# Computing a per-head denominator with 32-column tiles of the TensorE array, and issuing it later

## The chip, the cores and the metric

The kernel runs on one core of one Trainium2 chip. The metric is device time in microseconds (us). Lower is better. Engines are named as in the profile: PE is TensorE (matmul), PEld its weight loads, DVE is VectorE, ACT is ScalarE, POOL is GpSimd, SP is the engine whose queue issues the DMAs here.

## The reference, cut to what matters

One transformer block with linear attention and a gated feed-forward network, both added to the input. There are 2048 tokens, width 640, 32 heads of 20, feed-forward width 1728.

```python
pq, pk = phi(q), phi(k)                       # phi(t) = t+1 if t>0 else exp(t), + 1e-6
kv  = einsum("bhsd,bhse->bhde", pk, v)
z   = einsum("bhsd->bhd", pk)
num = einsum("bhqd,bhde->bhqe", pq, kv)
den = einsum("bhqd,bhd->bhq", pq, z)[..., None] + 1e-6     # <- one number per head and token
o   = num / den
out = x + o @ wo + (gelu(xn @ w_gate) * (xn @ w_up)) @ w_down
```

The change is about `den`: 32 numbers per token.

## The kernel before

The kernel has two phases. Phase 1 normalizes the tokens, computes k and v, accumulates `kv` and `z`, and computes most of q. A short phase boundary turns `kv` and `wo` into one matrix `M`. Phase 2 goes through four chunks of 512 tokens. A chunk has 13 GU tiles (10 matmuls of 512 columns each: gate and up projection), one smaller tile for the last 64 feed-forward columns (`u_ps`, 5 matmuls), and four OUT tiles (38 matmuls of 320 columns each), which trail by one chunk. The denominator (DEN) and its reciprocal are made in between and are broadcast over the heads through DRAM.

```python
# phi(q): relu part + exp part, done on DVE once per chunk
def emit_pq_combine(c, pin): ...
    for r_ap, e_ap in parts:                    # 5 tiles of pqT, then 40 rows of mix
        after(nc.vector.tensor_scalar(e_ap, e_ap, 1.0, PHI_EPS, op0=ALU.min, op1=ALU.add), pin, ...)
        nc.vector.tensor_tensor(r_ap, r_ap, e_ap, op=ALU.add)

def emit_DEN(c):
    cs = slice(c * CH, (c + 1) * CH)            # CH = 512
    den_ps = small_ps("den_ps")
    for t in range(NQF):                        # NQF = 5; zmat[:, t, :] is 128 columns wide, 32 of use
        nc.tensor.matmul(den_ps[:, :], lhsT=zmat[:QW, t, :], rhs=pqT[:QW, t, cs],
                         start=(t == 0), stop=False)
    nc.tensor.matmul(den_ps[:, :], lhsT=zmat5[:, :], rhs=mix[:, cs], start=False, stop=True)
    den_sb = work2.tile([H, CH], F32, tag="den_sb", name="den_sb", bufs=2)      # H = 32
    nc.scalar.activation(den_sb[:], den_ps[:H, :], ACT.Identity, bias=DEN_EPS)

# emit_recip: 4 pieces of 32 x 128 on DVE.  emit_BC_dma: one store of 1/den, then 8 broadcast loads.

# phase 2: small pieces of work are spread over the slots between GU tiles
if c == 0:
    rest.append(lambda: emit_pq_combine(0, pins["gu"]))
    rest.append(lambda: emit_DEN(0))
    rest += [(lambda p=p: emit_recip(0, p)) for p in range(NRP)]
    rest.append(lambda: emit_BC_dma(0))
if c + 1 < NCH:
    rest.append(lambda: emit_pq_combine(c + 1, pins["gu"]))
    rest.append(lambda: emit_DEN(c + 1))
    ...
```

A scheduler orders the emitted instructions on each engine. What counts is therefore the order that the trace shows, not the order of the code. (Where a text below speaks of the compiled program, the kernel of that run was built again, without the chip, and its instructions and waits were listed.)

## Time and profile before

| | before |
|---|---|
| time | 307.31 us median of 4 runs (306.52 to 308.31) |
| PE busy | 294.5 of 306.6 us |
| DEN matmuls on PE | 24 of 512 columns |
| PE idle recorded before DEN matmuls | 0.7 us |
| reciprocals on DVE | 16, mean 905 ns |

The busy table of the page for the kernel before (busy us, share of the span, number of instructions), and the first line of its chain of waits (the shares of the work that ended last):

```profile
PE 294.5 (96%) x1815; PEld 167.3 (55%) x1815; DVE 148.9 (49%) x303; ACT 92.4 (30%) x187; POOL 7.2 (2%) x32
...
PE 84%; DVE 10%; DMA 2%; ACT 2%; SPq 1%; issue 1%; DVEq 0%; ACTq 0%
```

TensorE bounds this kernel. DVE and ACT are idle at least half of the time.

The groups of instructions that the change touches. The columns are: line, engine, operation, output and inputs with their shapes, count | busy us, mean ns of one | idle us of the engine just before them and what ended most of it:

```profile
L435 PE MATMUL den_ps<-pqT,zmat 120*128 120x512 bf16 x20 | 7.3, 378 | 0.7 <-DVE pqT L347 0.7
L437 PE MATMUL den_ps<-mix,zmat 128*128 128x512 bf16 x4 | 1.5, 376 | 0.0
L439 ACT ACTIVATE den_sb<-den_ps 32x512 f32<-32x512 f32 x4 | 2.3, 587 | 8.5 <-PE den_ps L437 8.5
L448 DVE RECIPROCAL rden<-den_sb 32x128 bf16<-32x128 f32 x16 | 13.8, 905 | 1.1 <-ACT den_sb L439 1.1
```

A matmul of 512 columns is recorded as 378 ns, but that is its length from start to end, and matmuls overlap. The cost on a busy TensorE is the distance from one start to the next. The PE timeline around the first chunk's DEN shows this (start us, length us, engine, line, output and inputs, shapes, count, idle before):

```profile
103.23 0.38 PE L494 MATMUL gu<-xnT,wu_sb 128*128 128x512 bf16 x1
103.45 0.38 PE L491 MATMUL gu<-xnT,wg_sb 128*128 128x512 bf16 x1
104.00 0.38 PE L435 MATMUL den_ps<-pqT,zmat 120*128 120x512 bf16 x1 [0.17 <-DVE pqT L347]
104.21 0.38 PE L491 MATMUL gu<-xnT,wg_sb 128*128 128x512 bf16 x1
104.45 0.38 PE L437 MATMUL den_ps<-mix,zmat 128*128 128x512 bf16 x1
```

From 103.23 to 103.45 is 0.22 us, the price of 512 columns. (Five of them in a row take 1.08 us, so 216 ns each.) The DEN matmuls stand scattered between GU matmuls, each as soon as the scheduler expected its `pqT` tile to be ready.

### The profile page before, as it was taken

What the parts mean: (1) busy time and instruction counts of PE and PEld (TensorE: products, weight loads), DVE (VectorE), ACT (ScalarE), POOL (GpSimd) and SP (SyncE); (2) the same over time, 40 slices, a digit from 0 to 9 for tenths busy, and PEclk for the clock granted to TensorE, in tenths of its full rate; (3) what the DMA queues carried; (4) which work ended last, traced back from release to release, by engine and by line L of the source; (5) the groups of instructions that cost most, each with busy time, mean ns of one, the idle gap of its engine ahead of it and who ended that gap; (6) DMA issues with size and microseconds to landing.
All of it is one profiled execution on the core that took longest, in us unless ns stands there. A gap on an engine that the chain in (4) does not pass through costs nothing.

```text
span 306.6 us, 4493 instructions
## 1 busy us (share of the span) xinstructions
PE 294.5 (96%) x1815; PEld 167.3 (55%) x1815; DVE 148.9 (49%) x303; ACT 92.4 (30%) x187; POOL 7.2 (2%) x32
## 2 busy tenths in 40 slices
PE   6599999999989999999999999999999999999995
PEld 2256656566654444445655645466464564665773
DVE  5567867676354997678252239324223212223121
ACT  4245666575577322321021031201213012012000
POOL 3003200000000000000000000000000000000000
PEclk9989999999999999999999999999999999999999
DMA  7988970000002022132211010410100101101101
GB/s 221 269 308 285 240 275 24 21 2 0 0 2 65 0 52 45 29 57 70 60 50 43 0 44 2 126 45 8 43 27 18 43 2 43 41 4 43 43 24 43
DMA packets 17421, 20.81 MB, mean 68 GB/s; under 512 B 3513, under 2 KB 15481, under 8 KB 17401
## 3 DMA queue, kind: packets, MB, share of 16 engines
q1 hardware_dynamic: 17401, 20.54, 22.5%
q8 instruction: 14, 0.23, 0.3%
q14 instruction: 6, 0.05, 0.0%
HBM read 17.78 MB, written 2.75 MB: 67 GB/s over the span
## 4 chain that ended last, share of the span: by engine, by line
PE 84%; DVE 10%; DMA 2%; ACT 2%; SPq 1%; issue 1%; DVEq 0%; ACTq 0%
PE o_ps L520 26%; PE gu L494 16%; PE gu L491 16%; PE q_ps L317 7%; PE kp L280 6%; PE vp L280 5%; DVE pqT L347 2%; DMA x<-in_A_x_dram 2%; PE kp L281 1%; DVE hT L498 1%; PE u_ps L481 1%; PE kv_acc L302 1%; DVE eT L345 1%; PE vp L281 1%; PE tp L269 1%; PE q_ps L324 1%
## 5 line engine op out<-in xcount | busy, mean ns | idle before, releaser
L497 ACT ACTIVATE ge<-gu 128x512 bf16<-128x512 f32 x52 | 31.1, 597 | 138.8 <-PE gu L494 137.2
L498 DVE TENSOR_TENSOR hT<-ge,gu 128x512 bf16<-128x512 bf16 x52 | 35.4, 682 | 62.7 <-ACT ge L497 62.4
L491 PE MATMUL gu<-xnT,wg_sb 128*128 128x512 bf16 x260 | 65.4, 379 | 0.4 <-DVE M_sb L427 0.4
L494 PE MATMUL gu<-xnT,wu_sb 128*128 128x512 bf16 x260 | 65.4, 379 | 0.0
L520 PE MATMUL o_ps<-wd_sb,hT 128*128 128x320 bf16 x416 | 59.3, 299 | 0.0
L520 PEld LDWEIGHTS <-hT 128*128 128x128 bf16 x416 | 40.6, 98 | 16.1
L494 PEld LDWEIGHTS <-wu_sb 128*128 128x128 bf16 x260 | 25.4, 98 | 31.3 <-issue 1.0
L491 PEld LDWEIGHTS <-wg_sb 128*128 128x128 bf16 x260 | 25.4, 98 | 29.6 <-issue 1.2
L529 DVE TENSOR_TENSOR res<-o_ps,xr 128x640 bf16<-128x640 f32 x15 | 12.4, 825 | 51.5 <-PE o_ps L520 51.5
L280 PE MATMUL kp<-wqkv_sb,xnT 128*128 128x512 bf16 x80 | 24.9, 392 | 2.5 <-DMA wqkv_sb<-in_A_wqkv_dram 1.4
L520 PE MATMUL o_ps<-M_sb,pqT 120*128 120x320 bf16 x160 | 26.1, 299 | 0.6 <-DVE res L539 0.6
L280 PEld LDWEIGHTS <-xnT 128*128 128x128 bf16 x160 | 16.0, 100 | 18.1 <-issue 1.6
L280 PE MATMUL vp<-wqkv_sb,xnT 128*128 128x512 bf16 x80 | 24.0, 386 | 0.0
L317 PE MATMUL q_ps<-xnT,wqkv_sb 128*120 128x512 bf16 x100 | 23.9, 379 | 0.0
L520 PEld LDWEIGHTS <-pqT 120*128 120x128 bf16 x160 | 15.6, 97 | 10.3 <-issue 1.8
L281 PE MATMUL kp<-wqkv_sb,xnT 128*128 128x128 bf16 x80 | 18.0, 225 | 0.0
L281 PE MATMUL vp<-wqkv_sb,xnT 128*128 128x128 bf16 x80 | 17.7, 221 | 0.0
L281 PEld LDWEIGHTS <-xnT 128*128 128x128 bf16 x160 | 16.0, 100 | 3.1 <-issue 3.1
L317 PEld LDWEIGHTS <-wqkv_sb 128*120 128x120 bf16 x100 | 12.4, 133 | 7.6
L243 DVE BATCH_NORM_STATS2 stats<-x 128x6 f32<-128x320 bf16 x32 | 14.0, 480 | 4.3 <-DMA x<-in_A_x_dram 4.3
L448 DVE RECIPROCAL rden<-den_sb 32x128 bf16<-32x128 f32 x16 | 13.8, 905 | 1.1 <-ACT den_sb L439 1.1
L287 ACT ACTIVATE e_k<-kp 128x640 bf16<-128x640 f32 x16 | 11.2, 702 | 10.0 <-PE kp L281 9.9
(90 smaller groups left out, 219.1 us busy)
## 6 DMA issues: line engine op xcount, KB each, us to landing
x<-in_A_x_dram SPq DMA_DIRECT2D x16, 160.0 KB
xr<-in_A_x_dram SPq DMA_DIRECT2D x16, 160.0 KB
rb<-rden_d SPq DMA_DIRECT2D x24, 100.0 KB
out_dram<-res SPq DMA_DIRECT2D x15, 160.0 KB
wg_sb<-in_B_w_gate_dram SPq DMA_DIRECT2D x5, 416.0 KB
wu_sb<-in_B_w_up_dram SPq DMA_DIRECT2D x5, 416.0 KB
wd_sb<-in_B_w_down_dram SPq DMA_DIRECT2D x4, 480.0 KB
wqkv_sb<-in_A_wqkv_dram SPq DMA_DIRECT2D x5, 320.0 KB
```

Of the source, the lines that this page charges most:

```text
L243: ins = nc.vector.bn_stats(stats[:, j, :], x_t[:, j * h2:(j + 1) * h2])
L280: nc.tensor.matmul(dst[:, 0, :], lhsT, wqkv_sb[:, k, base:base + 512], start=st, stop=sp)
L281: nc.tensor.matmul(dst[:, 1, 0:rem], lhsT, wqkv_sb[:, k, base + 512:base + D], start=st, stop=sp)
L287: nc.scalar.activation(e[:], kflat, ACT.Exp)
L317: nc.tensor.matmul(q_ps[:QW, :], lhsT=wqkv_sb[:, k, t * QW:(t + 1) * QW], rhs=xnT[:, k, cs], start=(k == 0), stop=(k == KD - 1),)
L448: nc.vector.reciprocal(rden[:, c % 2, sl], den_sbs[c][:, sl])
L491: nc.tensor.matmul(gu[:, 0, :], lhsT=wg_sb[:, k, f * P:(f + 1) * P], rhs=xnT[:, k, cs], start=(k == 0), stop=(k == KD - 1))
L494: nc.tensor.matmul(gu[:, 1, :], lhsT=wu_sb[:, k, f * P:(f + 1) * P], rhs=xnT[:, k, cs], start=(k == 0), stop=(k == KD - 1))
L497: nc.scalar.activation(ge[:, :], gu[:, 0, :], ACT.Gelu_apprx_tanh)
L498: return nc.vector.tensor_tensor(hT[:, f, :], ge[:, :], gu[:, 1, :], op=ALU.mult)
L520: nc.tensor.matmul(o_ps[:, hf, 0:HB], lhsT=lhsT, rhs=rhs[:, hf * HB:(hf + 1) * HB], start=(n == 0), stop=(n == len(groups) - 1),)
L529: nc.vector.tensor_tensor(res[:].rearrange("p (a b) -> p a b", a=2), o_ps[:, :, 0:HB], xr[:].rearrange("p (a b) -> p a b", a=2), op=ALU.add,)
```

## The change

The intent is to waste less of the array on the denominator. DEN needs 32 output rows, but its stationary operand `zmat` is 128 columns wide, so 96 of the 128 output rows are of no use. The change narrows `zmat` to 32 columns, splits the chunk into four quarters of 128 tokens, and sends each quarter to another column tile of the array (`tile_position=(0, 32j)`), so that four matmuls can run side by side. The result then lies on 128 partitions, 128 wide, in place of 32 partitions, 512 wide, so the reciprocal on DVE has a quarter of the columns to go through. It is done in two pieces per chunk in place of four (`NRP`). Further, DEN is issued later (empty padding slots) and in one piece (a pin on the last combine of the chunk). Two more options, `EARLY_GU` and `WK_FIRST`, come with the change but are switched off; their code is cut here.

```diff
-    zmat = pers.tile([P, NQF, P], BF16, name="zmat")
-    zmat5 = pers.tile([P, P], BF16, name="zmat5")
-    rden = pers.tile([H, 2, CH], BF16, name="rden")
+    zmat = pers.tile([P, NQF, H], BF16, name="zmat")
+    zmat5 = pers.tile([P, H], BF16, name="zmat5")
+    NSUB = P // H
+    SW = CH // NSUB
+    rden = pers.tile([P, 2, SW], BF16, name="rden")
 ... (et, et5: the same narrowing; pq_combine: pins["combine"] = its last instruction)
     def emit_DEN(c):
-        for t in range(NQF):
-            nc.tensor.matmul(den_ps[:, :], lhsT=zmat[:QW, t, :], rhs=pqT[:QW, t, cs],
-                             start=(t == 0), stop=False)
-        nc.tensor.matmul(den_ps[:, :], lhsT=zmat5[:, :], rhs=mix[:, cs], start=False, stop=True)
-        den_sb = work2.tile([H, CH], F32, tag="den_sb", name="den_sb", bufs=2)
-        nc.scalar.activation(den_sb[:], den_ps[:H, :], ACT.Identity, bias=DEN_EPS)
+        for t in range(NQF + 1):
+            for j in range(NSUB):
+                cs = slice(c * CH + j * SW, c * CH + (j + 1) * SW)
+                if t < NQF:
+                    lhsT, rhs = zmat[:QW, t, :], pqT[:QW, t, cs]
+                else:
+                    lhsT, rhs = zmat5[:, :], mix[:, cs]
+                mm = nc.tensor.matmul(den_ps[j * H:(j + 1) * H, 0:SW], lhsT=lhsT, rhs=rhs,
+                                      start=(t == 0), stop=(t == NQF), tile_position=(0, j * H))
+                after(mm, pins["combine"], "keep the column-tiled matmuls contiguous")
+        den_sb = work2.tile([P, SW], F32, tag="den_sb", name="den_sb", bufs=2)
+        nc.scalar.activation(den_sb[:], den_ps[:, 0:SW], ACT.Identity, bias=DEN_EPS)
-    NRP = 4
+    NRP = 2
 ... (emit_BC_dma: four stores of 1/den in place of one)
         if c == 0:
             rest.append(lambda: emit_pq_combine(0, pins["gu"]))
+            rest += [lambda: None] * 5
             rest.append(lambda: emit_DEN(0))
         if c + 1 < NCH:
             rest.append(lambda: emit_pq_combine(c + 1, pins["gu"]))
+            rest += [lambda: None] * (3 if c == 0 else 1)
             rest.append(lambda: emit_DEN(c + 1))
```

More of the change, by code (lines that the diff above doesn't have):

```diff
@@ L20 @@
 DVE_RELU_EVERY = 2
+EARLY_GU = False
+WK_FIRST = False
 @with_exitstack
@@ L99, in load_x, with load_w @@
         return t
-    x_tiles[0] = load_x(0)
-    if NT > 1:
-        x_tiles[1] = load_x(1)
     wqkv_sb = work.tile([P, KD, 3 * D], BF16, name="wqkv_sb", bufs=1)
     wqkv_src = A_wqkv.rearrange("(k p) f -> p k f", p=P)
-    for k in range(KD):
-        nc.sync.dma_start(wqkv_sb[:, k, D:3 * D], wqkv_src[:, k, D:3 * D])
-    for i in range(2, min(4, NT)):
-        x_tiles[i] = load_x(i)
+    def load_w(col0, k0, k1):
+        nc.sync.dma_start(wqkv_sb[:, k0:k1, col0:col0 + D], wqkv_src[:, k0:k1, col0:col0 + D])
+    x_tiles[0] = load_x(0)
+    if WK_FIRST:
+        ksplit = min(KD, 2)
+        load_w(D, 0, ksplit)
+        if NT > 1:
+            x_tiles[1] = load_x(1)
+        if ksplit < KD:
+            load_w(D, ksplit, KD)
+        load_w(2 * D, 0, ksplit)
+        if NT > 2:
+            x_tiles[2] = load_x(2)
+        if ksplit < KD:
+            load_w(2 * D, ksplit, KD)
+        if NT > 3:
+            x_tiles[3] = load_x(3)
+    else:
+        if NT > 1:
+            x_tiles[1] = load_x(1)
+        for k in range(KD):
+            nc.sync.dma_start(wqkv_sb[:, k, D:3 * D], wqkv_src[:, k, D:3 * D])
+        for i in range(2, min(4, NT)):
+            x_tiles[i] = load_x(i)
     warm = const.tile([P, 512], BF16, name="warm")
@@ L180 @@
     kvmT = pers.tile([P, NQF + 1, P], BF16, name="kvmT")
-    zmat = pers.tile([P, NQF, P], BF16, name="zmat")
-    zmat5 = pers.tile([P, P], BF16, name="zmat5")
-    rden = pers.tile([H, 2, CH], BF16, name="rden")
+    zmat = pers.tile([P, NQF, H], BF16, name="zmat")
[3 more added lines that the diff above has]
+    rden = pers.tile([P, 2, SW], BF16, name="rden")
     rden_d = dram.tile([H, NCH, CH], BF16, name="rden_d")
-    et = const.tile([P, NQF, P], BF16, name="et")
-    et5 = const.tile([P, P], BF16, name="et5")
+    et = const.tile([P, NQF, H], BF16, name="et")
+    et5 = const.tile([P, H], BF16, name="et5")
     mask_bd = const.tile([P, HPT, DH], F32, name="mask_bd")
@@ L209, in deferred_const_pieces @@
         return [
-            seq(ms(et[:], 1.0), band(et[:], [[QW, NQF], [-DH, P]], 0, 1)),
+            seq(ms(et[:], 1.0), band(et[:], [[QW, NQF], [-DH, H]], 0, 1)),
             seq(ms(et5[:], 0.0), ms(et5[MO:MO + Q5, :], 1.0),
-                band(et5[MO:MO + Q5, :], [[-DH, P]], NQF * QW, 1)),
+                band(et5[MO:MO + Q5, :], [[-DH, H]], NQF * QW, 1)),
             seq(ms(mask_bd[:], 1.0), band(mask_bd[:], [[-DH, HPT], [0, DH]], 0, 1),
@@ L346, in emit_pq_combine @@
                   pin, "phi(q) combine belongs to phase 2")
-            nc.vector.tensor_tensor(r_ap, r_ap, e_ap, op=ALU.add)
+            last = nc.vector.tensor_tensor(r_ap, r_ap, e_ap, op=ALU.add)
+        pins["combine"] = last
     pending_q = deque()
@@ L356 @@
     late_w = deque(late_weight_pieces())
-    pins = {"kvp": None}
+    pins = {"kvp": None, "combine": None}
     for i in range(NT):
@@ L431, in emit_DEN @@
     def emit_DEN(c):
-        cs = slice(c * CH, (c + 1) * CH)
         den_ps = small_ps("den_ps")
-        for t in range(NQF):
-            nc.tensor.matmul(den_ps[:, :], lhsT=zmat[:QW, t, :], rhs=pqT[:QW, t, cs],
-                             start=(t == 0), stop=False)
-        nc.tensor.matmul(den_ps[:, :], lhsT=zmat5[:, :], rhs=mix[:, cs], start=False, stop=True)
-        den_sb = work2.tile([H, CH], F32, tag="den_sb", name="den_sb", bufs=2)
-        nc.scalar.activation(den_sb[:], den_ps[:H, :], ACT.Identity, bias=DEN_EPS)
+        for t in range(NQF + 1):
[3 more added lines that the diff above has]
+                    lhsT, rhs = zmat[:QW, t, :], pqT[:QW, t, cs]
+                else:
+                    lhsT, rhs = zmat5[:, :], mix[:, cs]
[4 more added lines that the diff above has]
+        nc.scalar.activation(den_sb[:], den_ps[:, 0:SW], ACT.Identity, bias=DEN_EPS)
         den_sbs[c] = den_sb
-    NRP = 4
+    NRP = 2
     def emit_recip(c, piece):
-        w = CH // NRP
+        w = SW // NRP
         sl = slice(piece * w, (piece + 1) * w)
-        with nc.allow_low_precision("1/den feeds a bf16 matmul operand"):
+        with nc.allow_low_precision("1/den feeds a bf16 multiply"):
             nc.vector.reciprocal(rden[:, c % 2, sl], den_sbs[c][:, sl])
@@ L452, in emit_BC_dma @@
     def emit_BC_dma(c):
-        nc.sync.dma_start(rden_d[:, c, :], rden[:, c % 2, :])
+        for j in range(NSUB):
+            nc.sync.dma_start(rden_d[:, c, j * SW:(j + 1) * SW], rden[j * H:(j + 1) * H, c % 2, :])
         rb = work2.tile([P, NQF + 1, CH], BF16, tag="rb", name="rb", bufs=1)
@@ L474, with emit_GU_mm @@
     hT_tiles = {}
+    gu_early = {}
+    def emit_GU_mm(c, f):
+        cs = slice(c * CH, (c + 1) * CH)
+        gu = big_ps("gu")
+        for k in range(KD):
+            nc.tensor.matmul(gu[:, 0, :], lhsT=wg_sb[:, k, f * P:(f + 1) * P], rhs=xnT[:, k, cs],
+                             start=(k == 0), stop=(k == KD - 1))
+        for k in range(KD):
+            nc.tensor.matmul(gu[:, 1, :], lhsT=wu_sb[:, k, f * P:(f + 1) * P], rhs=xnT[:, k, cs],
+                             start=(k == 0), stop=(k == KD - 1))
+        return gu
     def emit_GU(c, f):
@@ L485, in emit_GU @@
             return nc.vector.tensor_tensor(mix[:FL, cs], ge[:FL, :], u_ps[:FL, :], op=ALU.mult)
+        gu = gu_early.pop((c, f), None)
+        if gu is None:
+            gu = emit_GU_mm(c, f)
         if c not in hT_tiles:
@@ L488, in emit_GU @@
         hT = hT_tiles[c]
-        gu = big_ps("gu")
-        for k in range(KD):
-            nc.tensor.matmul(gu[:, 0, :], lhsT=wg_sb[:, k, f * P:(f + 1) * P], rhs=xnT[:, k, cs],
-                             start=(k == 0), stop=(k == KD - 1))
-        for k in range(KD):
-            nc.tensor.matmul(gu[:, 1, :], lhsT=wu_sb[:, k, f * P:(f + 1) * P], rhs=xnT[:, k, cs],
-                             start=(k == 0), stop=(k == KD - 1))
         ge = work2.tile([P, CH], BF16, tag="ge", name="ge", bufs=3)
@@ L552 @@
             boundary.pop(0)()
+        if n == 2 and EARLY_GU:
+            gu_early[(0, 0)] = emit_GU_mm(0, 0)
     ph1_stack.close()
```

## The prediction

> **What bounds the kernel.** TensorE. It is busy 294.5 of 306.6 us (96%, busy table), its granted clock is full after the start, and the chain that ended last is 84% PE. From 96 us to the output tail PE idles under 1 us (busy time by stretches). Matmuls follow each other at the rate of their columns: five of 512 columns fill 1.08 us (timeline), 216 ns each; those of 121 columns start about 60 ns apart. So only PE streaming and the few PE waits count. DVE (49%) and ACT (30%) have slack.
>
> **What it touches on PE.** EARLY_GU and WK_FIRST are off, so loads and GU are as before. The real change is the denominator: per 512-token chunk, 6 matmuls of 512 columns with 32 useful output rows become 24 of 128 columns on four column tiles.
> - Removed: 24 x 216 ns = 5.2 us, and the PE waits for the last combines (4 x 0.17 = 0.7 us). Padding slots and the pin put DEN about three GU tiles, or one OUT tile, after the combine, so I expect no wait there.
> - Added: 24 groups of four 128-column matmuls, each with its own 32-column weight load. The Trainium skill ("TensorE: Matmul & The Clock Gate", Part 3) says that column tiles run concurrently; "TensorEngine Tiling (Array Packing)" (Key Properties; Restrictions) says that a mode switch drains the array and that column tiling loses fast weight load. No trace here shows either yet. Perfectly concurrent, a group costs like one 128-column matmul, about 60 ns: 1.4 us in all. Fully serial, 240 ns: 5.8 us. I take about 120 ns, limited by four loads and issues: 2.9 us. Eight mode switches at up to a matmul's pipeline tail (376 ns recorded less 216 ns spacing = 160 ns): estimate 1.0 us.
> - Net on PE: 5.9 - 3.9 = about 2 us gained.
>
> **Off PE.** Reciprocals: 16 of 905 ns on 32x128 become 8 on 128x64, estimated 0.46 us each: 10 us less DVE, nearly none on the path. The ACT eviction shrinks from 587 ns to about 0.27 us. Three more stores per chunk, about 0.31 us issue each on the DMA queue, are offset by about 2 us less reciprocal; the broadcast tiles are needed slots later and showed no wait. At the phase boundary six zmat products (252 ns) shrink to 32 columns; PE waited 1.15 us there for the last: 0.1 to 0.5 us gained.
>
> **Predicted time.** 307.3 - 2.0 - 0.3 = 305.0 us; 8 in 10 between 302.6 and 307.2. Faster by over 2% (below 301.2): 0.04. Within 2%: 0.95. Slower by over 2%: 0.01.
>
> **What would show each step.**
> - DEN blocks contiguous, 24 matmuls each; from the first DEN matmul's start to the next GU or OUT matmul's start about 1.0 us (6 x 120 ns + two switches). Near 0.6 us means perfect concurrency; near 1.7 us serial execution.
> - Four matmuls of a group start within tens of ns of each other; gaps of some 0.1 us at block entry and exit.
> - PE waits on the pqT combine vanish.
> - DVE busy falls to about 138 us with no effect on the time; the reciprocals' mean is under 500 ns.
> - Wait of tpk on zmat falls from 1.15 us to under 1.0.
>
> **What would make it wrong.** Serial column tiles or slow weight loads (no gain, or 1 to 2 us lost); a semaphore wait on each of the 24 matmuls; the reordered schedule opening PE waits elsewhere, such as DVE standing at a broadcast tile that comes later than before and holding back PSUM; or a larger gain because the four tiles run fully together and switches cost nothing (about 302.5).

## The result, and the profile after

| | before | after |
|---|---|---|
| median | 307.03 us (16 runs, 306.38 to 308.31) | 302.54 us (11 runs, 301.29 to 303.85) |
| ratio | | 0.9844, 95% interval 0.9823 to 0.9866 |
| measured again on another occasion | 306.94 us | 302.26 us, ratio 0.9837 (0.9816 to 0.9859) |

A ratio is the mean time of one kernel's fast runs over that of the other's of the same rounds, so it isn't quite the ratio of the medians. The gain is 4.8 us by the ratio. The prediction said 2.3, and its range ended at 302.6, just above the measured median. So the direction was right, "within 2%" was right, and the size was wrong by a factor of two.

The same views of the kernel after, the busy table and the chain first:

```profile
PE 290.8 (97%) x1887; PEld 166.9 (55%) x1887; DVE 138.9 (46%) x295; ACT 90.6 (30%) x187; POOL 5.6 (2%) x32
...
PE 88%; DVE 5%; DMA 2%; ACT 2%; SPq 1%; issue 0%; DVEq 0%; ACTq 0%
```

The share of DVE in the chain fell from 10% to 5%: PE waits less for DVE. PE's busy time fell by only 3.7 us although the kernel gained more, because busy time counts the overlapping tails of matmuls too; don't read a gain from it.

The groups that answer to those shown of before:

```profile
L464 PE MATMUL den_ps<-pqT,zmat 120*32 120x128 bf16 x80 | 1.9, 221 | 0.0
L464 PE MATMUL den_ps<-mix,zmat 128*32 128x128 bf16 x16 | 0.9, 221 | 0.0
L468 ACT ACTIVATE den_sb<-den_ps 128x128 f32<-128x128 f32 x4 | 1.1, 271 | 0.0
L477 DVE RECIPROCAL rden<-den_sb 128x64 bf16<-128x64 f32 x8 | 3.8, 520 | 0.0
```

And the PE timeline at the second chunk's DEN:

```profile
112.55 1.24 PE L511 MATMUL gu<-xnT,wg_sb 128*128 128x512 bf16 x5
113.63 1.24 PE L514 MATMUL gu<-xnT,wu_sb 128*128 128x512 bf16 x5
114.80 0.46 PE L464 MATMUL den_ps<-pqT,zmat 120*32 120x128 bf16 x20
115.09 0.23 PE L464 MATMUL den_ps<-mix,zmat 128*32 128x128 bf16 x4
115.26 1.25 PE L511 MATMUL gu<-xnT,wg_sb 128*128 128x512 bf16 x5
```

The GU matmuls before the block would have let the next one start at 113.63 + 1.08 = 114.71. The next GU matmul starts at 115.26. So the block, with everything around it, costs 0.55 us. Three of the four blocks cost that, and the first one 0.73, with the extra 0.18 us after its last matmul. The sum is 2.37 us. The extra is a wait for DVE: the GU tile after the first block is the fifth, there are three large PSUM buffers, and so it needs the one that the multiplication of the second tile on DVE (`hT`) sets free. In the compiled program the tile's first matmul waits for this instruction alone. DVE gets to it only after chunk 0's combine, and it ends at 103.87; the GU matmul starts at 103.92. In the six profiles after, after again, e3, b2, b4 and b7 the start follows that end by 52 to 55 ns.

Read in single starts (from the trace, within a block), the four matmuls of a group start 3 to 4 ns apart, and the groups start at 0, 66, 122, 177, 233 and 289 ns, so 56 ns apart. Entering the block costs 93 ns and leaving it 97 ns beyond the columns' own time. In e1 below, whose DEN matmuls are as wide as those around them, three of the four blocks cost at most 10 ns to enter and 4 ns to leave, so the 190 ns go with the change of tile width.

### Where the time went

Single runs of the changed kernel differ by up to 2.6 us in the same state. The profiles show where executions of the same PE work differ: in the first 20 us, and at the very end. The profiles of after and of e3 are 0.83 us apart 21 us after the start and 0.77 us apart at the first GU matmul (94.56 and 95.33 us). In most profiles the granted clock falls to half once for 3.4 us, at 9 to 15 us after the start, in the kernel before as in the changed one. In the pair of profiles above the dip lies at 10.2 to 13.6 us in the changed kernel and at 14.4 to 17.8 us in the kernel before, and the changed kernel starts its first GU matmul 1.25 us earlier (94.56 against 95.81 us). I put this down to the dip: over all profiles, whatever the kernel, those with a dip before 11 us start the first standard GU matmul at 94.56 to 94.86 us, and those with a dip at 13.7 us or later at 95.02 to 95.81. No run tested it. The mean granted clock of a run doesn't sort the times: the changed kernel's three runs at 1.000 took 301.29 to 301.44 us and its others 302.0 to 303.9, but when it was measured again two runs at 1.000 took 302.09 and 302.26 us and one at 0.998 took 301.19.

The distance from the start of the first GU matmul to the start of the last matmul of the program leaves the beginning and the end out. Three profiles with the changed kernel's PE work (after, after again, e3) agree in it to 0.01 us, so I use it for all runs:

| run | first GU to last matmul, us | against before | median, us | ratio to before (95%) |
|---|---|---|---|---|
| before | 207.48 | | 307.03 | |
| after | 202.20 | -5.28 | 302.54 | 0.9844 (0.9823 to 0.9866) |
| after, again | 202.19 | -5.29 | 302.26 | 0.9837 (0.9816 to 0.9859) |
| e1 placement only | 205.64 | -1.84 | 304.97 | 0.9935 (0.9910 to 0.9959) |
| e2 tile by tile | 203.52 | -3.96 | 304.08 | 0.9896 (0.9875 to 0.9917) |
| e3 reciprocals thrice | 202.19 | -5.29 | 302.56 | 0.9847 (0.9826 to 0.9869) |
| e5 tiles scattered | 206.46 | -1.02 | 306.71 | 0.9991 (0.9968 to 1.0014) |
| e7 one tile | 206.06 | -1.42 | 306.06 | 0.9966 (0.9944 to 0.9987) |

The 5.28 us add up from what the two traces show. Before, DEN streamed 24 x 216 ns = 5.18 us. In addition, over the four DEN regions of the trace I summed the distance from each matmul's start to the next, less its columns' time, wherever more than 0.08 us was left: 0.63 + 0.43 + 0.69 + 0.70 = 2.45 us lost in short waits. After, there are 2.37 us of blocks and no such waits. 5.18 + 2.45 - 2.37 = 5.26. With the 0.26 us of the next paragraph taken off, 5.0 us are left, which lies within the interval of the ratio (4.1 to 5.4 us).

A part of this is given back at the end: from the last matmul's start to the end of the span, all profiles with one store of 1/den per chunk (before, e1, e7) show 3.28 us, and those with four stores show 3.53 to 3.55 (one of them 4.56). So 0.26 us at the end of the program go with the additional stores; whether and how they cause it was not tested.

### The profile page after: what moved, and what is told of

Same layout as the page of the kernel before. It is cut to its first block, busy times and chain, and to the rows that moved or that the text cites. A ratio compares the mean times of both kernels' runs of the same rounds, so it can differ in the third digit from the quotient of the medians.

```text
span 301.3 us, 4641 instructions
## 1 busy us (share of the span) xinstructions
PE 290.8 (97%) x1887; PEld 166.9 (55%) x1887; DVE 138.9 (46%) x295; ACT 90.6 (30%) x187; POOL 5.6 (2%) x32
## 4 chain that ended last, share of the span: by engine, by line
PE 88%; DVE 5%; DMA 2%; ACT 2%; SPq 1%; issue 0%; DVEq 0%; ACTq 0%
PE o_ps L558 27%; PE gu L511 18%; PE gu L514 18%; PE q_ps L340 7%; PE kp L303 5%; PE vp L303 5%; DMA x<-in_A_x_dram 2%; PE q_ps L347 1%; PE u_ps L523 1%; PE kv_acc L325 1%; PE kp L304 1%; PE vp L304 1%; PE tp L292 1%; DVE pk_buf L312 1%; DVE stats L266 1%; SPq L128 1%
## 5 line engine op out<-in xcount | busy, mean ns | idle before, releaser
L511 PE MATMUL gu<-xnT,wg_sb 128*128 128x512 bf16 x260 | 64.6, 379 | 0.5 <-DVE M_sb L451 0.4
L514 PE MATMUL gu<-xnT,wu_sb 128*128 128x512 bf16 x260 | 64.6, 379 | 0.0
L303 PE MATMUL kp<-wqkv_sb,xnT 128*128 128x512 bf16 x80 | 24.0, 380 | 2.3 <-DMA wqkv_sb<-in_A_wqkv_dram 1.5
L558 PE MATMUL o_ps<-M_sb,pqT 120*128 120x320 bf16 x160 | 24.5, 299 | 0.6 <-DVE res L577 0.6
L303 PE MATMUL vp<-wqkv_sb,xnT 128*128 128x512 bf16 x80 | 24.8, 395 | 0.0
L312 DVE SCALAR_TENSOR_TENSOR pk_buf<-kp,e_k 128x640 bf16<-128x640 f32 x16 | 13.2, 824 | 1.7
```

Source lines behind the costliest of these rows:

```text
L303: nc.tensor.matmul(dst[:, 0, :], lhsT, wqkv_sb[:, k, base:base + 512], start=st, stop=sp)
L312: last = nc.vector.scalar_tensor_tensor(pk_buf[:, vb, 0:D], in0=kflat, scalar=0.0, in1=e[:], op0=ALU.max, op1=ALU.add)
L511: nc.tensor.matmul(gu[:, 0, :], lhsT=wg_sb[:, k, f * P:(f + 1) * P], rhs=xnT[:, k, cs], start=(k == 0), stop=(k == KD - 1))
L514: nc.tensor.matmul(gu[:, 1, :], lhsT=wu_sb[:, k, f * P:(f + 1) * P], rhs=xnT[:, k, cs], start=(k == 0), stop=(k == KD - 1))
L558: nc.tensor.matmul(o_ps[:, hf, 0:HB], lhsT=lhsT, rhs=rhs[:, hf * HB:(hf + 1) * HB], start=(n == 0), stop=(n == len(groups) - 1),)
```

## The experiments

Theory T says that there are two halves: side-by-side tiles take DEN from 5.2 to 2.4 us, and the later, contiguous placement removes 2.4 us of short waits. The rivals: placement does it all (R1), or the relief of DVE does it (R2).

### e1: the placement without the tiles

The kernel before, with the padding and the pin, but DEN still six matmuls of 512 columns and the reciprocals as before:

```diff
+            mm = nc.tensor.matmul(den_ps[:, :], lhsT=zmat[:QW, t, :], rhs=pqT[:QW, t, cs], ...)
+            after(mm, pins["combine"], "contiguous")
 ...
+            rest += [lambda: None] * 5
             rest.append(lambda: emit_DEN(0))
 ...
+            rest += [lambda: None] * (3 if c == 0 else 1)
             rest.append(lambda: emit_DEN(c + 1))
```

> The kernel before, with the denominator still 6 matmuls of 512 columns per chunk and the old reciprocals, but with the padding slots and the pin on the combine, so that each chunk's 6 matmuls stand together at nearly the places where the changed kernel has its 24. Theory T (two halves: column tiles take the denominator's streaming from 5.2 us to about 2.4 us with mode switches, and the later placement takes away about 2.4 us of short PE stalls, 0.1 to 0.35 us each, that the idle figures show only in part): this run gains only the second half, so 2.0 to 2.6 us, about 304.8 us, ratio 0.992. Rival R1 (placement does it all): about 302.5 us, ratio 0.984. Rival R2 (the 10 us less work on DVE does it): about 307 us, ratio 1.00.

Measured: 304.97 us, ratio 0.9935, a gain of 2.0 us; 1.84 us in the distance of the table. Two parts of its PE timeline, the DEN of chunk 0 and that of chunk 1:

```profile
102.12 1.24 PE L497 MATMUL gu<-xnT,wu_sb 128*128 128x512 bf16 x5
103.21 1.25 PE L436 MATMUL den_ps<-pqT,zmat 120*128 120x512 bf16 x5
104.30 0.38 PE L439 MATMUL den_ps<-mix,zmat 128*128 128x512 bf16 x1
104.52 1.24 PE L494 MATMUL gu<-xnT,wg_sb 128*128 128x512 bf16 x5
...
115.31 0.38 PE L494 MATMUL gu<-xnT,wg_sb 128*128 128x512 bf16 x1
116.15 1.25 PE L436 MATMUL den_ps<-pqT,zmat 120*128 120x512 bf16 x5 [0.46 <-DVE mix L347]
```

At chunk 0 nothing is lost: 102.12 + 1.08 = 103.20, and DEN starts at 103.21. At chunk 1 one wait is left, 116.15 - 115.31 - 0.216 = 0.62 us, for DVE's combine. The other two chunks lose nothing. So the placement removes the 2.45 us and leaves 0.62 of a wait at one place, together 1.83, which is what was measured. R1 falls, since 3.4 of the 5.3 us are still missing: 2.8 are the tiles' (5.18 - 2.37), and 0.6 is this wait. The pin and the padding were not tried apart from each other.

The wait that is left belongs to a third part of the change. The scheduling code spreads its pieces evenly over the slots between GU tiles, and e1 keeps four reciprocal pieces per chunk where the changed kernel has two. Chunk 1's combine therefore comes one GU tile later here and ends 0.06 us before its DEN starts; in the changed kernel, and in e3 and e7, which have two pieces, it ends 1.47 us before. So some 0.6 us of the gain go with the smaller number of pieces. No run changed that number alone.

### e3: the reciprocals three times over

```diff
-            nc.vector.reciprocal(rden[:, c % 2, sl], den_sbs[c][:, sl])
+            for _ in range(3):
+                nc.vector.reciprocal(rden[:, c % 2, sl], den_sbs[c][:, sl])
```

> The changed kernel with each reciprocal done three times over, which puts back about 8 us of the 10 us of DVE work that the change took away, at the same place. Theory T (DVE is off the path): 302.5 us within 0.5, ratio 0.984 to 0.987. Rival R2 (relief of DVE gives part of the gain): slower by 1 to 3 us, ratio 0.988 to 0.994.

Measured: 302.56 us, ratio 0.9847, and the distance 202.19 us, that of the changed kernel to 0.01 us. Its busy table and the group of reciprocals:

```profile
PE 289.7 (96%) x1887; PEld 166.2 (55%) x1887; DVE 145.0 (48%) x311; ACT 90.7 (30%) x187; POOL 5.6 (2%) x32
...
L478 DVE RECIPROCAL rden<-den_sb 128x64 bf16<-128x64 f32 x24 | 10.4, 504 | 0.0
```

The reciprocals took 10.4 us in place of 3.8, somewhat less than the 8 us more that I had announced, and DVE was busy 145.0 us against 138.9. The time didn't move. R2 falls for this placement: the shorter time of the reciprocals is worth nothing here by itself. (e3 puts back 6.6 of the 10 us. e7 below, whose reciprocals take 13.7 us, has no wait outside its DEN blocks until the last OUT tile either. Both keep the two pieces per chunk, whose number matters, as e1 shows.)

### e2: the same matmuls in tile order

```diff
-        for t in range(NQF + 1):
-            for j in range(NSUB):
+        for j in range(NSUB):
+            for t in range(NQF + 1):
```

> The changed kernel with the two denominator loops swapped: same 96 matmuls, loads, places and mode switches, but all six of one column tile are issued before the next tile, so that neighbours in the stream use the same tile. Theory T (four tiles run at the same time, a group of four costs like one 128-column matmul): the streaming is serial now, 24 x 56 ns = 1.3 us per block in place of 0.35, so about +1.0 us per block, +3.9 us in all, about 306.4 us, ratio 0.997. Rival R1 (concurrency is not what matters): no change, 302.5 us, ratio 0.984.

Measured: 304.08 us, ratio 0.9896; 1.32 us more than the changed kernel in the distance, not the 3.9 that I expected, and not zero. The experiment didn't do what it was made for: the matmuls did not become serial. The timeline of one block (`mix` is the sixth and last matmul of each tile in program order):

```profile
115.74 0.48 PE L464 MATMUL den_ps<-pqT,zmat 120*32 120x128 bf16 x9
116.03 0.22 PE L464 MATMUL den_ps<-mix,zmat 128*32 128x128 bf16 x1
116.04 0.31 PE L464 MATMUL den_ps<-pqT,zmat 120*32 120x128 bf16 x5
116.15 0.22 PE L464 MATMUL den_ps<-mix,zmat 128*32 128x128 bf16 x1
116.17 0.29 PE L464 MATMUL den_ps<-pqT,zmat 120*32 120x128 bf16 x4
```

If matmuls started in program order, the `mix` matmuls would be the 6th, 12th, 18th and 24th to start. They are the 10th, 16th, 21st and 24th. The scheduler didn't mix them: in the program that this kernel compiles to, the 24 matmuls stand on PE tile by tile. So matmuls of the second tile started while the first tile still had some to come. The single starts fit four queues, one per tile: within a queue 56 ns from start to start, and each tile's first start 0.128 us after the one before, which is 21 ns for each of the six load-and-matmul pairs that go ahead of it. That the starts belong to the tiles in this way is my reading; the trace doesn't name the tile of a matmul. A block costs 0.92 us here.

### e7: the same matmuls on one tile

Here no two tiles can overlap: all 24 matmuls of a chunk go to tile (0, 0), the four quarters to four column ranges of the same 32 rows of PSUM. What follows on ACT and DVE is in the old shape; the trace shows no PE wait for it.

```diff
-                mm = nc.tensor.matmul(den_ps[j * H:(j + 1) * H, 0:SW], ...
-                                      start=(t == 0), stop=(t == NQF), tile_position=(0, j * H))
+                mm = nc.tensor.matmul(den_ps[0:H, j * SW:(j + 1) * SW], ...
+                                      start=(t == 0), stop=(t == NQF), tile_position=(0, 0))
```

(The loops are in the order of e2.)

> The changed kernel with the same 96 matmuls of 128 columns and 32-column loads at the same places, but all on one column tile (the four quarters of a chunk go to four column ranges of the same 32 rows of PSUM); what follows on ACT and DVE is as in the kernel before. The loop swap of an earlier run did not make the matmuls serial (its blocks took 0.92 us: matmuls of later tiles started while earlier tiles still had some waiting), so here overlap is impossible. Theory T: 24 x 56 ns = 1.34 us of streaming and 0.2 us of switching per block, 1.54 in place of 0.55 us, +3.9 us in all, about 306.4 us, ratio 0.997. If overlap between tiles is not what saves the time: 302.5 us, ratio 0.985.

Measured: 306.06 us, ratio 0.9966; 3.86 us more than the changed kernel in the distance. The first block:

```profile
102.50 1.24 PE L513 MATMUL gu<-xnT,wu_sb 128*128 128x512 bf16 x5
103.67 0.45 PE L464 MATMUL den_ps<-pqT,zmat 120*32 120x128 bf16 x5
103.96 0.22 PE L464 MATMUL den_ps<-mix,zmat 128*32 128x128 bf16 x1
104.02 0.44 PE L464 MATMUL den_ps<-pqT,zmat 120*32 120x128 bf16 x5
104.30 0.22 PE L464 MATMUL den_ps<-mix,zmat 128*32 128x128 bf16 x1
...
105.13 0.39 PE L510 MATMUL gu<-xnT,wg_sb 128*128 128x512 bf16 x1
```

Six matmuls of one quarter take 104.02 - 103.67 = 0.35 us, then come the next six. With four tiles all 24 took this time. The block costs 105.13 - (102.50 + 1.08) = 1.55 us against 0.55. The array works on the four tiles at once, and this is worth 3.9 us, measured with as many matmuls of the same size at nearly the same places. (The order of the loops differs too. Against e2, which has e7's order and differs on PE by the tiles alone, e7's distance is 2.54 us longer.)

### e5: the tiles without padding and pin

```diff
-            rest += [lambda: None] * 5
-            rest += [lambda: None] * (3 if c == 0 else 1)
-                after(mm, pins["combine"], "keep the column-tiled matmuls contiguous")
```

> The changed kernel without the padding and without the pin: the scheduler then spreads the column-tiled matmuls in fours between GU and OUT matmuls, 23 blocks in place of 4, at the early places that the kernel before had. Theory T (a change of tiling mode costs about 0.19 us for entry and exit together, a group of four about 0.05 us): 19 more entries and exits cost 19 x 0.19 = 3.6 us; the short stalls before may partly hide in them. About 305.5 to 307.5 us, ratio 0.995 to 1.001. If switches cost next to nothing: 302.5 to 304.5 us.

Measured: 306.71 us, ratio 0.9991. The gain is gone. The scheduler places the matmuls in 23 blocks, nearly all of four, as soon as their `pqT` tile is expected:

```profile
101.12 0.38 PE L513 MATMUL gu<-xnT,wu_sb 128*128 128x512 bf16 x1
101.52 0.24 PE L464 MATMUL den_ps<-pqT,zmat 120*32 120x128 bf16 x4
101.70 0.39 PE L513 MATMUL gu<-xnT,wu_sb 128*128 128x512 bf16 x1
102.02 0.24 PE L464 MATMUL den_ps<-pqT,zmat 120*32 120x128 bf16 x4
102.19 0.82 PE L513 MATMUL gu<-xnT,wu_sb 128*128 128x512 bf16 x3
```

Between the GU matmul at 101.70 and the one at 102.19 lie 0.49 us, of which the GU matmul's columns take 0.216 and the DEN group's 0.056. The other 0.22 us are the entry and the exit, which I put down to the two changes of tile width. Against the changed kernel there are 19 more blocks, and the distance is 4.27 us longer: 0.22 us for each. So the entry and the exit are not free; four blocks of 24 pay them four times, 23 blocks of four pay away the whole gain of the tiles. It also shows that the halves don't simply add: the tiles alone gain 1.0 us in the distance, the placement alone 1.8, both together 5.3, mostly because tiles pay only in one piece (the 0.6 us of the wait that e1 kept is in the difference too).

### c1: the changed kernel again

> The changed kernel again, as the yardstick for the other three on the same chip: 302.5 us within 0.5, ratio 0.984 to 0.987. Its profile shows whether the 1.2 us longer wait for the last store in the first profile of the changed kernel belongs to it or varies: theory T says that it varies, 2.4 to 3.7 us after the last addition.

Measured: 302.26 us, ratio 0.9837, and 3.54 us from the last matmul's start to the end, where the first profile had 4.56. That long end varied, as T said (2.71 us after the last addition here, 3.73 in the first profile). (This trace lacks 28 of 1887 matmul records, and those of e7, b2, b4, b7 and b5 lack some too; starts and distances quoted from them avoid the gaps.)

### Faster versions: b2, b4, b7, b5

If a column tile pays here, it pays elsewhere: the last 64 feed-forward columns (`u_ps`) fill half of the array. b2 gives them two tiles of 64:

```diff
-                nc.tensor.matmul(u_ps[:, :], lhsT=wmixU[:, k, :], rhs=xnT[:, k, cs], ...)
+                for j in range(2):
+                    nc.tensor.matmul(u_ps[j * MO:(j + 1) * MO, 0:HC], lhsT=wmixU[:, k, 0:MO],
+                                     rhs=xnT[:, k, c * CH + j * HC:c * CH + (j + 1) * HC], ...
+                                     tile_position=(0, j * MO))
 ... (the product with gelu(gate) is taken in two halves of 256 columns)
```

> The changed kernel, with the same idea on the up projection's last 64 columns: per chunk, 5 matmuls of 512 columns with 64 useful rows become 10 of 256 columns on two 64-row column tiles, and the product is taken in two halves. Theory T: 5 pairs at [...]109 ns plus 0.2 us of switching = 0.74 us in place of 1.08, 0.34 us per chunk, 1.3 us in all: about 301.2 us, ratio to before 0.980. If two 64-row tiles do not overlap: 5 x 2 x 109 + 200 = 1.3 us, 0.8 us slower than the changed kernel, 303.3 us.

Measured: 300.90 us, ratio 0.9800 (0.9776 to 0.9824), distance 200.97, 1.23 us less than the changed kernel. (The expectation's 109 ns for 256 columns are about half of the 216 ns that 512 columns take.) One of its four places in the timeline:

```profile
124.03 1.24 PE L514 MATMUL gu<-xnT,wu_sb 128*128 128x512 bf16 x5
125.20 0.74 PE L525 MATMUL u_ps<-xnT,wmixU 128*64 128x256 bf16 x10
125.87 0.82 PE L511 MATMUL gu<-xnT,wg_sb 128*128 128x512 bf16 x2
```

125.87 - (124.03 + 1.08) = 0.76 us for what took five matmuls of 216 ns before, 1.08 us. The sizes learned from DEN (columns at full rate, 0.2 us per block) carried over.

b4 adds two edits against waits that the spacing of the matmuls shows: the halves of the last OUT tile get PSUM buffers of their own, and every second query tile at the phase boundary uses the large PSUM buffers.

```diff
+                oh = small_ps("oh")           # last OUT tile: one per half, in place of o_ps[:, hf]
 ...
-        q_ps = small_ps("q_ps")
+        q_ps = big_ps("q_ps")[:, 0, :] if big else small_ps("q_ps")
```

> The same, and two of the stalls taken away that the spacing of the matmuls shows: the last output tile's halves get PSUM buffers of their own (0.74 us in which PE waits for the first half's addition), and every second query tile of the phase boundary uses the large PSUM buffers that are free by then (1.3 us before the transposes). From theory T: 1.3 + 0.7 + up to 1.3 us off the changed kernel's time, about 299.5 us, between 299 and 301, ratio 0.973 to 0.980. If idle TensorE time of this kind were hidden elsewhere: 301.2 us, as the run with the up projection alone.

Measured: 300.59 us, ratio 0.9791 (0.9767 to 0.9815), inside the range but 1.1 us above the 299.5. The distance is 200.23: the 0.74 us wait in the last OUT tile is gone. The boundary gained nothing: its wait came back elsewhere, as two lines of the PE timeline show,

```profile
84.58 0.44 PE L432 MATMUL tpk<-ident,kvm 120*120 120x120 bf16 x5
...
92.22 0.38 PE L446 MATMUL m_ps<-wo_sb,kvmT 120*120 120x512 bf16 x1 [0.88 <-ACT M_sb L449]
```

with no bracket at the transposes any more, but a new one at the M matmuls. From the last `kv` matmul to the first GU matmul it takes 11.79 us, against 11.72 in every profile with the old boundary. b7 therefore leaves the boundary alone and keeps the other two edits:

> The changed kernel with the up projection's last columns on two column tiles and with separate PSUM buffers for the halves of the last output tile, but with the query tiles at the phase boundary as they were. The distance from the first GU matmul to the last matmul should be 200.2 us, as in the run with all three edits (200.23), and the time up to the first GU matmul only about 0.14 us longer than there at the same clock, because the trace of that run showed the wait before the transposes (1.31 us) come back as waits between the M matmuls (1.04, 0.35 us). Theory: 300.3 us within 0.5, ratio 0.976 to 0.981, no difference from the run with all three that the noise lets see.

Measured: 299.48 us, ratio 0.9759 (0.9729 to 0.9789), distance 200.22. This is the fastest version, 2.4% under the kernel before. It came out 0.3 us under the range that I expected, and below b4; the intervals of the two ratios overlap, and there are few runs of each, so I don't claim that the boundary edit costs more than the 0.07 us of the two traces.

b5 is b7 with the switch `EARLY_GU = True`, which moves the first GU tile into the boundary.

> The same with the change's own switch EARLY_GU on: the first GU tile's 10 matmuls are issued between the query tiles and the transposes at the phase boundary, where PE stood for 1.31 us before the transposes and 0.53 us before the first GU matmul. If there is work to fill these waits with, the boundary gets 1.3 to 1.8 us shorter, 298.5 to 299 us, ratio about 0.972. If ACT bounds the boundary (9.1 of 12 us busy there), the waits only move: 299.5 to 300.5 us, ratio 0.976 to 0.980.

Measured: 300.58 us, ratio 0.9785 (0.9758 to 0.9812). Nothing was gained: from the last `kv` matmul to the start of the second GU tile it takes 14.92 us, against 13.88 in b7. The M matmuls, whose PSUM buffers the early GU tile now shares, wait for their evictions:

```profile
93.91 0.38 PE L446 MATMUL m_ps<-wo_sb,kvmT 120*120 120x512 bf16 x1 [0.34 <-ACT M_sb L449]
...
96.12 0.38 PE L446 MATMUL m_ps<-wo_sb,kvmT 120*120 120x512 bf16 x1 [1.20 <-DVE M_sb L451]
```

## Why the prediction was right or wrong

**TensorE bounds, DVE doesn't: right in the main.** DVE busy fell from 148.9 to 138.9 us (138 was predicted), reciprocals fell to a mean of 520 ns (under 500 was predicted, a near miss), and e3 shows that the length of this work is off the path. At two places DVE does hold PE up: 0.18 us after the first block, and 0.62 us in e1. The prediction listed waits that the new order opens elsewhere among its risks; the 0.18 us are one.

**"Removed: ... the PE waits for the last combines (4 x 0.17 = 0.7 us)": this step failed.** The waits around DEN cost 2.45 us. The bracket of the timeline and the idle column of the groups count idle time from a matmul's recorded end, 160 ns after the next could have started, and waits shorter than that don't appear at all. The prediction had both numbers, 376 ns and 216 ns, and even their difference, but used it only for the switches. The DEN matmuls met 13 such waits, of which it counted four. e1 shows the waits by themselves: 1.84 us gained by placement alone, with one wait of 0.62 us still open.

**"I take about 120 ns, limited by four loads and issues: 2.9 us. Eight mode switches ... estimate 1.0 us": this step failed too.** A group took 56 ns, what one 128-column matmul takes in e7, so 24 groups cost 1.35 us. The 24 weight loads of a block overlap with the matmuls and were no limit. The switches measured 93 + 97 = 190 ns per block, 0.76 us for four. The wait of 0.18 us after the first block, and 20 ns per block by which the starts inside it spread beyond 6 x 56 ns, make the sum 2.37 us against 3.9 predicted. The prediction named the case of perfect concurrency and what would show it ("near 0.6 us"; 0.55 was measured), but took a value between this case and serial execution, a limit by loads and issues that no trace had shown.

The two terms were 1.75 and 1.5 us off, in the same direction. With the right sizes the sum is 5.3 us on PE.

**"At the phase boundary ... 0.1 to 0.5 us gained": wrong, 0.0.** From the last `kv` matmul to the first GU matmul it takes 11.72 us in both kernels. The products did get shorter, 252 to 232 ns. But the transposes never waited for them; the prediction took over the name that the profile gives. The PE line of before with ACT's `g_last`, then the PE line of after:

```profile
86.97 0.57 ACT L337 COPY g_last<-q_ps 64x512 f32<-64x512 f32 x1
87.58 0.43 PE L408 MATMUL tpk<-ident,kvm 120*120 120x120 bf16 x5 [1.15 <-DVE zmat L401]
```

```profile
86.33 0.43 PE L432 MATMUL tpk<-ident,kvm 120*120 120x120 bf16 x5 [1.15 <-ACT g_last L360]
```

In the kernel before, the last `zmat` product (87.53 us) and `g_last` (87.54 us) end almost together, and the profile names the wrong one. The transposes read `ident` and `kvm`, not `zmat`. They need one of the small PSUM buffers, which `g_last` frees, and in both compiled programs the first transpose waits for `g_last` alone; in both traces it starts 0.05 us after its end. That b4's larger buffers took this wait away fits with it.

**"DEN blocks contiguous ... waits on the pqT combine vanish": right**, all four blocks of 24, no wait.

**Not foreseen:** the 0.26 us at the end that goes with the four stores per chunk.

## What to carry to other kernels

Where TensorE bounds, measure its waits from start to start of neighbouring matmuls against the time of their columns; busy shares and idle brackets leave out the first 0.16 us of every wait here, the matmul's tail, and so 24 scattered matmuls lost 2.45 us where 0.7 us were recorded. A matmul with 32 or 64 useful output rows can be split over column tiles and then costs its columns divided by the number of tiles plus about 0.2 us per block here, so gather such matmuls into few blocks, behind data that is certainly ready. Where two instructions end almost at the same time, the profile may name the wrong one as what ended a wait; ask whether the waiting instruction reads what is named, or needs its buffer, before counting on a gain.

## What the Trainium skill lacked or had wrong

- "TensorE: Matmul & The Clock Gate", Part 3 (What overlaps and what doesn't) says that matmuls are "pc-monotone in start AND end — strict FIFO, no reordering". In e2 the 6th, 12th, 18th and 24th matmul of a block in the compiled order were the 10th, 16th, 21st and 24th to start. Across column tiles the order of starts was not the program's.
- The same page, Part 3, gives about 4 ns from start to start across tiles; the trace agrees (3 to 4 ns). But its Part 1 says that the distance "never drops below ≈25 ns"; this doesn't hold across column tiles. Its speedup for column tiles is 2.38 for three tiles of 512 columns. Four tiles of 128 columns measured 4.0 on the columns (56 ns per group against four times 56 ns in e7), and 2.8 with the switches (1.55 against 0.55 us per block).
- The same page (Back-to-back issue gap) gives about 131 ns as the sustained distance of 512-column matmuls with their weight loads. The GU streams here, each matmul with its own weight load, run at 216 ns at the full granted clock, the page's figure for the isolated gap.
- "TensorEngine Tiling (Array Packing)", Key Properties, says that a change of the tiling mode drains the array, with no figure. Measured: 93 ns on entry and 97 ns on exit in blocks of 24, and 0.22 us per block in e5's small ones. Both ways together are not much more than one matmul's tail of 160 ns.
- The same page, Restrictions, says that column tiling turns fast weight load off. No harm from it was visible: 24 loads of 32 columns took 0.34 us in a block, beside 24 matmuls that started within 0.30 us, and the groups followed each other at 56 ns.
- "Perfetto Trace Analysis", Identifying the Most-Contended Engine, says that the matmul busy share is no good measure of the distance to the limit, because matmuls are pipelined. The traces agree: PE's busy time fell by 3.7 us where the stretch from the first GU matmul to the last matmul got 5.3 us shorter. The page lacks the other side, that idle time before a matmul is too short in the same way: here 0.7 us of recorded idle time stood for 2.45 us of lost issue time.
